# Giving the weight words and the first 26 value products PSUM tiles of their own

## The chip, the cores and the metric

The kernel runs on one core of a Trainium2 chip. The metric is the device time of one launch in microseconds (us); the time before is 849.8 us, the median of three runs (849.23 to 850.05). A difference of 0.2%, about 1.7 us, is roughly what a measurement of this kernel can tell from no change.

## The reference, cut to what matters

The reference is an attention layer followed by a dense layer with a maximum of three products.

```python
# 8 batches, 8 heads, 512 local and 32 global tokens, head size 64
s_g = scale * q_g @ k_all.T;  out_g = softmax(s_g) @ v_all        # global rows see all 544 keys
s_l = concat(scale * q_l @ k_g.T, where(|i-j| <= 32, scale * q_l @ k_l.T, -1e9))
out_l = softmax(s_l) @ concat(v_g, v_l)                           # local rows: globals and a window
x = concat(out_g, out_l) reshaped to 4352 tokens x 512
h = maximum(maximum(x @ w1, x @ w2), x @ w3)                      # 512 -> 768
out = h @ w_out                                                   # 768 -> 512
```

## The kernel before, in words

**Attention by tiles.** A pair of heads has four tiles of 128 local queries; 8 batches times 4 pairs times 4 tiles make 128 tiles. The first 16 are batch 0, taken by halves: `ORDER` (L29) has the first two tiles of all four pairs ahead of the last two of all four. The main loop (L545) makes one tile a turn: `scores` (L325) multiplies queries and keys, takes the mask and the minimum on VectorE (L355), the exponential on ScalarE (L357), and normalises (`times`, L107: L114 on VectorE, L116 on ScalarE, L118 on GpSimd); `trans` (L368) transposes the probabilities on TensorE (L376) into the PSUM tile `T`, which has one buffer, and `copy` (L99: L103 on VectorE, L105 on ScalarE) moves them to `pt`; `glob`, `glob_soft` and `transg` (L279, L303, L387) do the same for the 32 global queries, whose transposed piece is the TensorE instruction `S<-ident,probg` (L394); `pv` (L404) multiplies with the values into the PSUM tile `O` and copies the product to `xr`. The first 26 tiles (`NAT`) use plain float32 operands (L417); later ones use operands split in a high and a low part (L424).

**The dense layer.** `moe_group` (L447) multiplies tokens with weights in split form: `xs` times `wh` and `wl` (L463), the maximum on VectorE (L471), then the high and low part of `h` times `woh` and `wol` (L482). It is a generator; `fill` (L512) takes a few of its matmuls between the steps of a tile. Batch 0 is done in two groups of 256 tokens, the later batches in groups of 512. The first group needs the first eight tiles, the second the next eight.

**The weight pieces.** The weights come as 64-bit floats in 24 pieces of 128 x 512. `convert` (L150) takes a piece through six steps: a DMA into `wraw` (L153, three buffers), the absolute value of the high word on ScalarE (L158, into `wct`), a clamp on GpSimd (L161), three integer operations on VectorE that put together the float32 word (L165, L166, L167), the high part on ScalarE (L170, `wh` or `woh`), the low part on GpSimd (L173, `wl` or `wol`). `weight_step` moves each live piece on by one step. In program order one or two such steps stand in each of the first 18 turns (`WS`, L510).

**Where the words live.** The PSUM pool `psO` has one buffer of 128 x 2 x 512 floats, two halves of 512 columns. It is taken once at the start as `early_o` (L140). L165 and L166 write its second half as the scratch of the words, and L166 and L167 read it. In the same tile, `pv` of the first 18 tiles (`EARLY_O`) writes the first half, in three thirds of 160 columns by turn (L408). From tile 18 on `pv` takes a new `O` of the whole size.

**What sets the order.** The program is written once, in program order; a scheduler then puts each engine's instructions in a fixed row, moving an instruction ahead of others where its operands, as the scheduler sees them, allow, and sets the waits between engines. It follows operands by tile, so what is written in one tile stays in program order there. On the chip each engine works off its row in order and waits where a semaphore says so.

Of the kernel before, what the change touches and what calls it, by code (L numbers as in the profile page):

```python
# [10 lines left out]
F32 = mybir.dt.float32  # L11
F32R = mybir.dt.float32r
I32 = mybir.dt.int32
# [4 lines left out]
PSUM = bass.MemoryType.PSUM  # L18
# [32 lines left out]
def f32(ap):  # L51
    return ap.bitcast(F32)


def body(ctx, tc, kin, qin, vin, min_, win, out):
    nc = tc.nc
    act, dve, pool, pe = nc.scalar, nc.vector, nc.gpsimd, nc.tensor
# [5 lines left out]
    pm = ctx.enter_context(tc.tile_pool(name="pm", bufs=3, space=PSUM))  # L63
    psS = ctx.enter_context(tc.tile_pool(name="psS", bufs=2, space=PSUM))
    psT = ctx.enter_context(tc.tile_pool(name="psT", bufs=1, space=PSUM))
    psO = ctx.enter_context(tc.tile_pool(name="psO", bufs=1, space=PSUM))

    small = ctx.enter_context(tc.tile_pool(name="small", bufs=4))


    load = {"a": 0.0, "d": 0.0, "p": 0.0}

    def width(ap):
        n = 1
        for x in ap.shape[1:]:
            n *= x
        return n

    def spend(e, ns):
        load[e] += ns  # L80

    def least(costs):
        e = min(costs, key=lambda e: load[e] + costs[e])
        load[e] += costs[e]
        return e
# [13 lines left out]
    def copy(out, a, psum=False):  # L99
        n = width(out)  # L100
        c = {"d": n * (1.04 if psum else 0.52) + (160 if psum else 150), "a": n * 0.833 + (150 if psum else 190)}
        if least(c) == "d":
            dve.tensor_copy(out=out, in_=a)  # L103
        else:
            act.copy(out=out, in_=a)  # L105
# [31 lines left out]
    xg = const.tile([128, NP, B, SG], F32, name="xg")  # L137


    early_o = psO.tile([128, 2, 512], F32, name="O")  # L140

    def pieces():
        for n in range(24):
            f, i = divmod(n, 3)
            if n < 18:
                yield n, *[w[f][:, i].rearrange("p k f -> p (k f)") for w in (wh, wl)]
            else:
                yield n, *[w[:, n - 18] for w in wo]

    def convert(piece):  # L150
        m, dh, dl = piece
        r = moe.tile([128, 512], mybir.dt.int64, name="wraw", tag=f"h{3 + m % 3}")
        nc.sync.dma_start(out=r, in_=win[m])  # L153
        hi = r.bitcast(I32).rearrange("p (n t) -> p n t", t=2)[:, :, 1]
        lo = r.bitcast(I32).rearrange("p (n t) -> p n t", t=2)[:, :, 0]
        yield
        c = att.tile([128, 512], I32, name="wct", tag="vs") if m % 2 else moe.tile([128, 512], I32, name="wct", bufs=2)
        act.activation(out=f32(c), in_=r.bitcast(F32).rearrange("p (n t) -> p n t", t=2)[:, :, 1], func=AF.Abs)  # L158
        spend("a", 620)
        yield  # L160
        pool.tensor_scalar(out=f32(c), in0=f32(c), scalar1=HIMAX, scalar2=2.0 ** -15, op0=ALU.min, op1=ALU.max)  # L161
        spend("p", 800)
        yield
        w = early_o[:, 1].bitcast(I32)
        dve.tensor_scalar(out=w, in0=c, scalar1=0x07FFFFFF, scalar2=3, op0=ALU.bitwise_and, op1=ALU.logical_shift_left)  # L165
        dve.scalar_tensor_tensor(out=w, in0=hi, scalar=-0x40000000, in1=w, op0=ALU.bitwise_and, op1=ALU.bitwise_or)  # L166
        dve.scalar_tensor_tensor(out=c, in0=lo, scalar=29, in1=w, op0=ALU.logical_shift_right, op1=ALU.bitwise_or)  # L167
        spend("d", 2000)
        yield
        act.copy(out=dh, in_=f32(c))  # L170
        spend("a", 615)
        yield
        pool.tensor_tensor(out=dl, in0=f32(c), in1=f32(dh), op=ALU.subtract)  # L173
        spend("p", 1290)
        yield True
# [5 lines left out]
    def weight_load():  # L181
        piece = next(todo, None)
        if piece is not None:
            c = convert(piece)
            next(c)
            loaded.append(c)
# [11 lines left out]

    NAT = 26
    EARLY = 16  # L200
    EARLY_O = 18
    kraw, kst, qraw, qs, vraw, vs, xr, sc, pg, pts, pgt = [{} for _ in range(11)]
    prob = []
    kn, qg = [], []
# [199 lines left out]
    def pv(sl):  # L404
        p, t = divmod(ORDER[sl], 4)
        pt = pts.pop(sl)
        if sl < EARLY_O:
            o = early_o[:, :, 160 * (sl % 3):160 * (sl % 3) + 160]  # L408
        else:
            o = psO.tile([128, 2, 512], F32, name="O")  # L410
        if t == 0:
            xr[p] = xp.tile([128, 4, 160], F32, name="xr")
        if sl < NAT:

            for c, j in ((0, 0), (0, 1), (1, 0), (1, 1)):
                n = 160 if c < GCH[t][2] else 128
                pe.matmul(o[64 * j:64 * j + 64, 0, 0:n], lhsT=vraw[sl][:, 2 * j + c], rhs=pt[:, j, c, 0:n], start=(c == 0), stop=(c == 1))  # L417
            copy(xr[p][:, t], o[:, 0, 0:160], True)
        else:

            for j in range(2):
                for c in range(2):
                    n = 160 if c < GCH[t][2] else 128
                    pe.matmul(o[:, j, 0:320].rearrange("p (a q) -> p a q", a=2)[:, :, 0:n],  # L424
                              lhsT=vs[sl][:, 2 * j + c].rearrange("p a d -> p (a d)"),
                              rhs=pt[:, j, c, :, 0:n], start=(c == 0), stop=(c == 1))
            lo = att.tile([64, 2, 160], F32, name="lox", bufs=1)
            copy(lo, o[64:128, :, 0:160], True)
            spend("d", 460 + 2 * 320)
            dve.tensor_tensor(out=lo, in0=o[0:64, :, 160:320], in1=lo, op=ALU.add)  # L430
            for j in range(2):
                dve.tensor_tensor(out=xr[p][64 * j:64 * j + 64, t], in0=o[0:64, j, 0:160], in1=lo[:, j], op=ALU.add)  # L432
        if t == 3:
            dve.tensor_reduce(out=xg[:, p % NP, p // NP], in_=xr[p][:, :, 128:160].rearrange("p t g -> p g t"),
                              axis=AX.X, op=ALU.add)
# [109 lines left out]
    for sl in range(NS):  # L545
        p, t = divmod(ORDER[sl], 4)
# [9 lines left out]
        n = (7, 6, 5, 9) if sl < 16 else (4, 4, 3, 7)  # L556
# [9 lines left out]
        elif sl == 15:  # L566
            load_k(6)
        fill(n[1])
        pv(sl)
        if sl < 8:  # L570
            if p < 3:
# [87 lines left out]
```

## Time and profile before

| | |
|---|---|
| Median of three runs | 849.8 us |
| The profiled execution | 850.82 us, of which the span is 848.8 us |
| TensorE busy | 814.9 us (96%) |
| VectorE, ScalarE, GpSimd busy | 523.8, 530.4, 515.4 us (62, 62, 61%) |
| TensorE idle from 215 us to 840 us | 0.0 us |

The profile names engines PE (TensorE matmuls), PEld (its weight loads), DVE (VectorE), ACT (ScalarE), POOL (GpSimd), SP (the queue that issues DMAs). `L417` is line 417 of the kernel printed above. In a row `[1.99 <-ACT wh L170]` says that the engine sat idle for 1.99 us before this instruction and that a ScalarE instruction of line 170 ended the wait; `x4` counts instructions merged into a row, and a float32 matmul counts twice.

### The profile page before, as it was taken

Reading aid. Unit: us, or ns where it says so; the run is one execution under the profiler, and the core shown is the slowest. Engines: PE = TensorE matmul, PEld = TensorE weight load, DVE = VectorE, ACT = ScalarE, POOL = GpSimd, SP = SyncE. Lnnn points to the kernel's source line nnn. Section 1 sums busy time; section 2 is a strip of 40 time slices with the busy share of each in tenths; the row PEclk is TensorE's granted clock in tenths of the full one; section 3 lists DMA queues with packets and bytes.
Section 4 is the critical chain, followed back from the end, with each engine's and each line's share of the span. In section 5 each row is a group of like instructions: output and inputs, shape, how many; then the busy total and the mean of one; then the engine's idle time right before and its main releaser. Section 6 shows DMA issues by size and latency. Waiting matters only on the chain.

```text
span 848.8 us, 15999 instructions
## 1 busy us (share of the span) xinstructions
PE 814.9 (96%) x4668; PEld 685.8 (81%) x4668; DVE 523.8 (62%) x1784; ACT 530.4 (62%) x1498; POOL 515.4 (61%) x727
## 2 busy tenths in 40 slices
PE   7769889899999999999999999999999999999997
PEld 4558758888888888888888888888888888888896
DVE  4667754677677676767777677676776766421111
ACT  6667665776776777766776776777776676411111
POOL 4677755686768666766678766866676674411211
PEclk9779999999999999999999999999999999999999
DMA  7455545434333433353333433253335322100001
GB/s 262 143 171 190 183 138 150 139 107 146 97 110 94 150 102 101 104 163 113 100 102 114 139 110 109 83 156 100 109 107 161 103 79 72 58 13 1 25 25 26
DMA packets 93415, 94.58 MB, mean 111 GB/s; under 512 B 18448, under 2 KB 81808, under 8 KB 93328
## 3 DMA queue, kind: packets, MB, share of 16 engines
q1 hardware_dynamic: 93328, 93.56, 35.7%
q8 instruction: 38, 0.62, 0.3%
q14 instruction: 49, 0.40, 0.2%
HBM read 56.85 MB, written 8.91 MB: 77 GB/s over the span
## 4 chain that ended last, share of the span: by engine, by line
PE 81%; DVE 2%; DMA 1%; ACT 1%; POOL 1%; issue 1%; SPq 0%; POOLq 0%; ACTq 0%; DVEq 0%
PE pm L463 47%; PE pm L482 15%; PE O L424 6%; PE S L352 5%; PE T L376 4%; PE S L295 2%; DMA prob<-s 1%; PE S L394 1%; PE O L417 1%; PE S L348 1%; ACT s L357 0%; DVE xr L432 0%; DVE pt L97 0%; ACT sg L308 0%; DVE s L355 0%
## 5 line engine op out<-in xcount | busy, mean ns | idle before, releaser
L463 PE MATMUL pm<-xs,wh 128*128 128x512 f32 (+1 forms) x1440 | 419.9, 367 | 2.7 <-ACT wh L170 2.4
L463 PEld LDWEIGHTS pm<-xs,wh 128*128 128x128 f32 x1440 | 252.6, 189 | 33.3 <-ACT wh L170 2.9
L463 PE MATMUL pm<-xs,wl 128*128 128x512 f32 (+1 forms) x720 | 266.0, 370 | 3.9 <-POOL wl L173 3.8
L463 PEld LDWEIGHTS pm<-xs,wl 128*128 128x128 f32 x720 | 136.1, 189 | 25.7 <-POOL wl L173 5.2
L118 POOL TENSOR_SCALAR s<-s,z 128x224 f32<-128x224 f32 (+1 forms) x246 | 105.6, 442 | 63.8 <-ACT lox L105 40.6
L482 PE MATMUL pm<-woh,h 128*128 128x512 f32 x408 | 133.9, 399 | 1.0 <-POOL h L97 1.0
L357 ACT ACTIVATE s<-s,nm 128x224 f32<-128x224 f32 (+1 forms) x256 | 118.2, 463 | 18.8 <-DVE nm L355 14.5
L97 POOL TENSOR_TENSOR h<-m,h 128x512 fp32r<-128x512 f32 (+1 forms) x60 | 68.7, 1145 | 99.0 <-ACT h L105 98.7
L471 DVE TENSOR_TENSOR m<-pm,m 128x512 f32<-128x512 f32 (+1 forms) x120 | 73.0, 608 | 77.6 <-PE pm L463 75.5
L97 POOL TENSOR_TENSOR qs<-qraw,qs 128x256 fp32r<-128x256 f32 x100 | 73.2, 740 | 62.6 <-ACT qs L105 54.3
L97 DVE TENSOR_TENSOR pt<-T,pt 128x512 fp32r<-128x512 f32 x102 | 70.5, 691 | 63.2 <-ACT pt L105 61.9
L355 DVE CUSTOM_DVE_ANT_0 s<-S,mask 128x224 f32<-128x224 f32 (+1 forms) x240 | 80.6, 371 | 30.2 <-PE S L348 23.8
L482 PEld LDWEIGHTS pm<-woh,h 128*128 128x128 f32 x408 | 74.3, 188 | 13.7 <-POOL h L97 1.6
L482 PE MATMUL pm<-wol,h 128*128 128x512 f32 x204 | 82.3, 404 | 2.5 <-POOL wol L173 2.5
L97 POOL TENSOR_TENSOR vs<-vraw,vs 128x256 fp32r<-128x256 f32 x102 | 75.8, 744 | 6.5 <-ACT vs L105 3.3
L97 POOL TENSOR_TENSOR kst<-kraw,kst 64x576 fp32r<-64x576 f32 x50 | 71.6, 1433 | 13.2 <-issue 6.3
L105 ACT CAST pt<-T 128x512 fp32r<-128x512 f32 x88 | 51.3, 583 | 40.7 <-PE T L376 40.6
L105 ACT CAST qs<-qraw 128x256 fp32r<-128x256 f32 x99 | 40.2, 407 | 53.6 <-PE S L352 52.0
L424 PEld LDWEIGHTS O<-pt,vs 128*128 128x128 f32 x408 | 66.1, 188 | 8.8
L424 PE MATMUL O<-pt,vs 128*128 128x320 f32 (+1 forms) x408 | 72.8, 300 | 0.0
L432 DVE TENSOR_TENSOR xr<-O,lox 64x160 f32<-64x160 f32 x204 | 64.3, 315 | 3.4
L352 PEld LDWEIGHTS S<-kst,qs 128*128 128x128 f32 x400 | 59.5, 190 | 8.5 <-DVE nmg L299 0.2
(97 smaller groups left out, 1228.1 us busy)
## 6 DMA issues: line engine op xcount, KB each, us to landing
vraw<-v_in SPq DMA_DIRECT2D x64, 256.0 KB, 3.2
qraw<-q_in SPq DMA_DIRECT2D x100, 128.0 KB, 2.2
prob<-s SPq DMA_DIRECT2D x56, 224.0 KB, 2.4
wraw<-w_in SPq DMA_DIRECT2D x24, 512.0 KB, 3.4
prob<-s SPq DMA_DIRECT2D x56, 192.0 KB, 2.3
out_dram<-o SPq DMA_DIRECT2D x32, 256.0 KB, 2.5
kraw<-k_in SPq DMA_DIRECT2D x25, 320.0 KB, 3.0
qn<-q_in SPq DMA_DIRECT2D x8, 256.0 KB, 6.0
```

What stands on the lines that cost most here:

```text
L97: (dve if least(c) == "d" else pool).tensor_tensor(out=out, in0=a, in1=b, op=ALU.subtract)
L105: act.copy(out=out, in_=a)
L118: pool.tensor_scalar(out=out, in0=a, scalar1=col, scalar2=1.0, op0=ALU.mult, op1=ALU.mult)
L352: pe.matmul(ph[j][:, 0:n], lhsT=qs[i][:, a, 128 * j:128 * j + 128], rhs=kst[p][:, j, c0:c0 + n], start=(a == 0), stop=(a == 1))
L355: dve.tensor_tensor_reduce(out=s[:, j, 0:n], in0=ph[j][:, 0:n], in1=mask[:, (1, 0, 1, 0)[t], 32 * (t == 0):32 * (t == 0) + n], scale=-0.12 ...
L357: act.activation(out=s[:, j, 0:n], in_=s[:, j, 0:n], func=AF.Exp, bias=nm[:, j:j + 1], scale=-1.0, accum_out=ze[:, j, 0:1])
L376: pe.transpose(pr[:, 256 * j + 128 * c:256 * j + 128 * c + 128], s[:, j, 128 * c:128 * c + 128], one)
L424: pe.matmul(o[:, j, 0:320].rearrange("p (a q) -> p a q", a=2)[:, :, 0:n], lhsT=vs[sl][:, 2 * j + c].rearrange("p a d -> p (a d)"), rhs=pt[ ...
L432: dve.tensor_tensor(out=xr[p][64 * j:64 * j + 64, t], in0=o[0:64, j, 0:160], in1=lo[:, j], op=ALU.add)
L463: pe.matmul(ps[:, 0:n], lhsT=w[f][:, i, k], rhs=xs[k][:, a, c0:c0 + n], start=(q == 0), stop=(q == 11))
L471: dve.tensor_tensor(out=m[:, 0:n], in0=ps[:, 0:n], in1=m[:, 0:n], op=ALU.max)
L482: pe.matmul(ps, lhsT=hh[f][:, a, 128 * t:128 * t + 128], rhs=w[:, f], start=(q == 0), stop=(q == 17))
```

## The change

The pool `psO` and the tile `early_o` go from the start of the program. A pool `psE` takes their place, with two tiles of one buffer each: `W`, 128 x 512 integers, taken anew by every weight piece, and `O`, 128 x 160 floats, taken anew by `pv` of each of the first 26 tiles. Each takes one PSUM bank (the place of a 512-column float32 tile, of which `psO` took two). At tile 26 `psE` is closed and `psO` is opened in its place for the later tiles. So the value products no longer go round three thirds of one bank but take one place by turn, and no tile is shared with the words. Instructions, operands, DMAs and the engine on which each stands are the same in number and shape; their order in the rows of the engines is not. Lines after the edit shift by one or two (L463 is L465 after, L417 is L419).

```diff
-    psO = ctx.enter_context(tc.tile_pool(name="psO", bufs=1, space=PSUM))
+    first = ctx.enter_context(ExitStack())
+    psE = first.enter_context(tc.tile_pool(name="psE", bufs=1, space=PSUM))
+    psO = []
...
-    early_o = psO.tile([128, 2, 512], F32, name="O")
...
-        w = early_o[:, 1].bitcast(I32)
+        w = psE.tile([128, 512], I32, name="W")
         dve.tensor_scalar(out=w, in0=c, scalar1=0x07FFFFFF, scalar2=3, op0=ALU.bitwise_and, op1=ALU.logical_shift_left)
...
-        if sl < EARLY_O:
-            o = early_o[:, :, 160 * (sl % 3):160 * (sl % 3) + 160]
-        else:
-            o = psO.tile([128, 2, 512], F32, name="O")
+        if sl < NAT:
+            o = psE.tile([128, 160], F32, name="O")
+        else:
+            if not psO:
+                first.close()
+                psO.append(ctx.enter_context(tc.tile_pool(name="psO", bufs=1, space=PSUM)))
+            o = psO[0].tile([128, 2, 512], F32, name="O")
...
-                pe.matmul(o[64 * j:64 * j + 64, 0, 0:n], lhsT=vraw[sl][:, 2 * j + c], rhs=pt[:, j, c, 0:n], start=(c == 0), stop=(c == 1))
-            copy(xr[p][:, t], o[:, 0, 0:160], True)
+                pe.matmul(o[64 * j:64 * j + 64, 0:n], lhsT=vraw[sl][:, 2 * j + c], rhs=pt[:, j, c, 0:n], start=(c == 0), stop=(c == 1))
+            copy(xr[p][:, t], o, True)
```

On TensorE the rows of the two programs differ between the first group's first matmuls and the product of tile 20; from there to the end they are the same, instruction for instruction. The rows below, in the prediction, show three places of the difference.

More of the change, by code (lines that the diff above doesn't have):

```diff
@@ L200, in body @@
     EARLY = 16
-    EARLY_O = 18
     kraw, kst, qraw, qs, vraw, vs, xr, sc, pg, pts, pgt = [{} for _ in range(11)]
```

## The prediction

> **What bounds the kernel now.** I read the page first, then the stretches, who waited for whom, and the timelines of the engines in the stretches that came out. The page's busy line and its clock row:
>
> ```profile
> span 848.8 us, 15999 instructions
> PE 814.9 (96%) x4668; PEld 685.8 (81%) x4668; DVE 523.8 (62%) x1784; ACT 530.4 (62%) x1498; POOL 515.4 (61%) x727
> PEclk9779999999999999999999999999999999999999
> ```
>
> PE bounds the whole, and the clock dips only in the second and third slice. The stretches, with PE's busy time as the second number and the granted clock as the one behind the last engine:
>
> ```profile
> 21.00:45.20 24.20, 15.98 (x79) 11.13 (x80) 16.03 (x57) 15.30 (x46) 15.95 (x29) 0.75 0.49 150
> 45.20:64.00 18.80, 14.31 (x76) 11.16 (x77) 11.00 (x35) 12.55 (x38) 13.00 (x20) 0.77 0.55 172
> 64.00:85.00 21.00, 20.61 (x165) 18.50 (x164) 15.54 (x41) 14.57 (x39) 16.93 (x23) 1.00 0.57 187
> 85.00:95.00 10.00, 9.24 (x67) 7.91 (x66) 8.21 (x24) 7.36 (x19) 7.44 (x11) 1.00 0.55 168
> 95.00:106.00 11.00, 8.79 (x62) 6.96 (x61) 7.41 (x23) 7.16 (x20) 7.47 (x10) 1.00 0.65 199
> 106.00:119.00 13.00, 10.81 (x57) 6.86 (x54) 9.54 (x25) 8.38 (x23) 8.30 (x10) 1.00 0.56 180
> 119.00:127.00 8.00, 7.05 (x51) 4.39 (x53) 1.80 (x10) 5.37 (x14) 3.46 (x5) 1.00 0.21 63
> 127.00:148.00 21.00, 20.85 (x172) 18.47 (x169) 10.05 (x49) 11.89 (x40) 10.97 (x17) 1.00 0.52 156
> 215.00:840.00 625.00, 625.00 (x3448) 532.12 (x3446) 386.05 (x1293) 386.65 (x1078) 372.82 (x511) 1.00 0.31 95
> ```
>
> From 215 us on PE is never idle, and the changed order meets the old one at the product of tile 20 (about 131 us). So the change is worth what PE gains before 131 us, one for one. What there is to gain: idle of 8.2 us (24.20 - 15.98) from 21 to 45, 4.5 (18.80 - 14.31) to 64, 0.4 to 85, and 6.1 from 85 to 127. To this comes the clock: 30.3 us of PE work (15.98 + 14.31) at 0.76 would be about 23 at 1.00, 7.2 us more. All together some 26 us; ahead of 21 us the two orders differ hardly. Who is waited for, in the first 260 us:
>
> ```profile
> PE S L394 <- POOL probg L118: 4.2, 2, 2.5
> PE pm L463 <- POOL wl L173: 3.8, 5, 1.2
> PE pm L482 <- POOL wol L173: 2.5, 5, 0.9
> PE pm L463 <- ACT wh L170: 2.4, 2, 2.0
> PE T L376 <- ACT pt L105: 1.9, 3, 1.3
> PE O L417 <- DVE wct L167: 1.4, 2, 1.1
> ```
>
> Weight pieces that come late (8.7 us in three rows) cost more than the products that wait for a piece's words (1.4, the last row).
>
> **First place: the first words.** VectorE, from the transposed piece of pair 1 on (`pt<-S`), before:
>
> ```order
> L103 COPY pt<-S 128x2x32 [waits PE_49]
> L360 RECIPROCAL z<-z 128x2 [waits DVE_49]
> L299 ISA sg,nmg<-S,zero 64x384 [waits PE_49,Pool_49]
> L299 ISA nmg 64x1
> L359 TENSOR_REDUCE z<-z_92 128x2 [waits Activation_49]
> L299 ISA sg,nmg<-S,zero 64x160 [waits PE_49]
> L299 ISA nmg 64x1
> L165 TENSOR_SCALAR O<-wct 128x512 [waits Activation_49]
> ```
>
> VectorE in the new order, where the first words stand ahead of tile 6's scores (L354) and of all of the above:
>
> ```order
> L165 TENSOR_SCALAR W<-wct 128x512 [waits Pool_49]
> L354 ISA s_94,nm<-pm,mask 128x192 [waits PE_49]
> L354 ISA nm 128x1
> L358 TENSOR_REDUCE z<-z_92 128x2 [waits Activation_49]
> L105 COPY pt<-T 128x4x128 [waits PE_49]
> L359 RECIPROCAL z<-z 128x2 [waits DVE_49]
> L105 CAST xs<-xr 128x256 [waits Activation_49]
> L308 TENSOR_SCALAR zg<-zg 64x1 [waits Activation_49]
> L354 ISA s_94,nm<-pm,mask 128x192
> L354 ISA nm 128x1
> L309 RECIPROCAL zg<-zg 64x1 [waits DVE_49]
> L166 SCALAR_TENSOR_TENSOR W<-wraw,W 128x512 [waits DMAHW1_49]
> ```
>
> The wait on ScalarE (the copy out of `O`) is gone, and the words moved 24 rows up. The trace has the clamped piece long before it is used (POOL, DVE, and what PE waits for behind it):
>
> ```profile
> 18.51 0.61 POOL L161 TENSOR_SCALAR wct<-wct 128x512 f32<-128x512 f32 x1
> 27.02 0.68 DVE L165 TENSOR_SCALAR O<-wct 128x512 int32<-128x512 int32 x1
> 29.85 0.79 PE L463 MATMUL pm<-xs,wh 128*128 128x256 f32 x2 [1.99 <-ACT wh L170]
> 31.21 0.58 PE L463 MATMUL pm<-xs,wl 128*128 128x256 f32 x1 [0.57 <-POOL wl L173]
> 41.43 0.39 PE L463 MATMUL pm<-xs,wl 128*128 128x256 f32 x1 [1.16 <-POOL wl L173]
> 45.13 0.48 PE L394 MATMUL S<-ident,probg 128*128 128x128 f32 x1 [2.51 <-POOL probg L118]
> ```
>
> The clamp ends at 19.1 and L165 starts at 27.0: the first piece can be some 5 us earlier, so I cost the waits of 1.99, 0.57 and 1.16 at nothing afterwards: -3.7. The price stands on GpSimd, whose row up to the normalised global probabilities of pair 2 was, before:
>
> ```order
> L118 TENSOR_SCALAR s_94<-s_94,z 128x224 [waits DVE_49,Activation_49]
> L118 TENSOR_SCALAR s_94<-s_94,z 128x224 [waits Activation_49]
> L173 TENSOR_TENSOR wl_104<-wct,wh_98 128x512 [waits Activation_49]
> L118 TENSOR_SCALAR probg<-sg,zg 64x128 [waits DVE_49,Pool_49]
> L118 TENSOR_SCALAR probg<-sg,zg 64x96 x2
> ```
>
> and is now, from the same piece 0's low part on:
>
> ```order
> L173 TENSOR_TENSOR wl_104<-wct,wh_98 128x512 [waits Activation_49]
> L99 TENSOR_TENSOR xs<-xr,xs 128x256 [waits Activation_49]
> L161 TENSOR_SCALAR wct<-wct 128x512 [waits Activation_49]
> L173 TENSOR_TENSOR wl_104<-wct,wh_98 128x512 [waits DVE_49,Activation_49]
> L120 TENSOR_SCALAR s_94<-s_94,z 128x224 [waits DVE_49,PE_49]
> L120 TENSOR_SCALAR s_94<-s_94,z 128x224 [waits PE_49]
> L120 TENSOR_SCALAR probg<-sg,zg 64x128 [waits DVE_49,Pool_49]
> L120 TENSOR_SCALAR probg<-sg,zg 64x96 x2
> ```
>
> An `xs`, a clamp and a second low part moved ahead of `probg`, which PE's `S<-ident,probg` waits for. Their durations:
>
> ```profile
> 35.78 0.61 POOL L161 TENSOR_SCALAR wct<-wct 128x512 f32<-128x512 f32 x1 [1.64 <-ACT wct L158]
> 36.36 0.74 POOL L97 TENSOR_TENSOR xs<-xr,xs 128x256 fp32r<-128x256 f32 x1
> 32.88 1.26 POOL L173 TENSOR_TENSOR wl<-wct,wh 128x512 fp32r<-128x512 f32 x1 [0.73 <-ACT wh L170]
> ```
>
> 0.61 + 0.74 + 1.26 = 2.6 us. PE has work moved ahead of that wait (below), but it runs out: I charge all 2.6. The 2.51 us at 45.13 has the same chain behind it, and I leave it. First term: **-3.7 + 2.6 = -1.1 us**, bounds +2.6 (nothing saved) and -6.2 (1.99 + 0.57 + 1.16 + 2.51, all gone and the price hidden).
>
> **Second place: the products.** TensorE behind the global piece of pair 1, before (`O_113` is `early_o`, the product that of tile 3):
>
> ```order
> L376 MATMUL T_429<-ident_82,s4_94 128x128 [waits Activation_49]
> L376 MATMUL T_429<-ident_82,s4_94 128x128 x3
> L463 MATMUL pm_657<-xs_314,wh0_98 128x256 [waits Activation_49]
> L463 MATMUL pm_657<-xs_314,wh0_98 128x256
> L463 MATMUL pm_657<-xs_314,wl0_104 128x256 [waits Pool_49]
> L394 MATMUL S_413<-ident_82,probg_405 128x128 [waits Activation_49,Pool_49]
> L348 MATMUL S_436<-kn_114,qn_243 128x224 [waits DMAHW5_49,PE_49]
> L348 MATMUL S_436<-kn_114,qn_243 128x224
> L417 MATMUL O_113<-pt_322,vraw_181 64x160 [waits DVE_49]
> ```
>
> and now (`O_400` is the same product):
>
> ```order
> L465 MATMUL pm_674<-xs_315,wh0_98 128x256 [waits Activation_49]
> L465 MATMUL pm_674<-xs_315,wh0_98 128x256
> L465 MATMUL pm_674<-xs_315,wl0_104 128x256 [waits Pool_49]
> L375 MATMUL T_435<-ident_82,s4_94 128x128 [waits Activation_49]
> L375 MATMUL T_435<-ident_82,s4_94 128x128
> L419 MATMUL O_400<-pt_323,vraw_180 64x160 [waits Activation_49]
> L419 MATMUL O_400<-pt_323,vraw_180 64x160 x3
> ```
>
> The product moved ahead of pair 2's global piece, and waits for the copy out of `O` in place of the words on VectorE. What the old wait cost, and what came of it:
>
> ```profile
> 55.50 0.71 PE L417 MATMUL O<-pt,vraw 128*64 128x160 f32 x8 [1.12 <-DVE wct L167]
> 57.53 1.12 PE L376 MATMUL T<-ident,s 128*128 128x128 f32 x4 [1.31 <-ACT pt L105]
> ```
>
> The second wait is the first's child: the copy of `pt` stands on ScalarE behind the copy out of `O`. Second term: 1.12 + 1.31 + 0.28 (the rest of the 1.4 above) = **-2.7 us**; if the copy out of `O` is late in place of the words, 0.
>
> **The clock.** The same four half-products, with the idle time before them:
>
> ```profile
> 45.40 1.70 PE L348 MATMUL S<-kn,qn 128*128 128x224 f32 x4
> 51.55 0.93 PE L348 MATMUL S<-kn,qn 128*128 128x224 f32 x4
> ```
>
> Right behind the 2.51 us wait they take 1.70 us, six microseconds later 0.93: after waits of this size PE runs at half speed for some 4 us. Four waits bring these 7.2 us (the two for `probg`, 4.2 in all, that at 29.85 and those at 55 to 57); two of them go, one new one comes on `probg`: a quarter, **-1.8 us**; bounds 0 and -7.2. The Trainium skill, "TensorE: Matmul & The Clock Gate", Part 1 (the HAM clock gate), throttles after an idle window of about 3.4 us; no single wait here is that long and the slow matmuls are there all the same, so the measurement decides. By the page's figure alone this term would be 0 and the sum 1.8 us smaller.
>
> **The later weight pieces.** Between 64 and 215 us PE waits for pieces like this:
>
> ```profile
> PE pm L482 <- POOL wol L173: 2.5, 5, 0.9
> PE pm L463 <- POOL wl L173: 2.0, 3, 1.0
> PE pm L463 <- ACT wh L170: 0.4, 1, 0.4
> ```
>
> Together 4.9 us. The pieces come in pairs between two products. First words of the pairs' first pieces, and the last piece's last:
>
> ```profile
> 61.40 0.70 DVE L165 TENSOR_SCALAR O<-wct 128x512 int32<-128x512 int32 x1 [0.80 <-POOL wl L173]
> 99.18 0.69 DVE L165 TENSOR_SCALAR O<-wct 128x512 int32<-128x512 int32 x1 [0.92 <-ACT xr L105]
> 119.65 0.68 DVE L167 SCALAR_TENSOR_TENSOR wct<-wraw,O 128x512 int32<-128x512 int32 x1
> ```
>
> Ten pieces lie between the first two rows, 3.8 us a piece, and the second shows the words waiting for the copy out of `O`. Without that tie GpSimd is next: in 64 to 85 us, 5.5 pieces at this pace, it is 16.93 us busy, 3.1 a piece. Over the last 15 pieces 0.7 us each would cover all 4.9 us; a pace that stays covers none. I take half: **-2.5 us**.
>
> **New waits.** Freed rows make new ones: half a wait of the largest size seen, 2.51: **+1.2 us** (0 to 2.5). At tile 26 the new pool waits for copies that are long done: nothing.
>
> Sum: -1.1 - 2.7 - 1.8 - 2.5 + 1.2 = **-6.9 us**, so the profiled execution's 850.8 (its span of 848.8 and 2.0 around it) would be 843.9; it lies 1.0 above the median of the runs, and the median of 849.8 becomes **842.9**.
>
> **The rivals.** *The tie was the whole lock.* If the early waits go too (-6.2), the products' (-2.7), half the clock (-3.6) and all weight waits (-4.9), with one new wait of 2.5, it is -14.9: 834.9; from half of what is beyond my forecast on, about -10, I count it here. For it: between 21 and 127 us no engine is full. Against: GpSimd is 81% busy in the best stretch. Chance 0.20. *The tie hides behind the pieces.* PE gets its work at the pace of the pieces, and their pace is that of the chain of DMA and five engine steps: then the last two terms give nothing and the clock little: -0.5 to -4, around 847.5. For it: direct waits on the words are 1.4 us only. Chance 0.20. *Slower: weight work ahead of `probg`.* GpSimd and VectorE now take words first, and PE's row stops at `S<-ident,probg`, with everything queued behind. If both such waits (pairs 2 and 3) grow by 2.6 us, each brings 4 us at half speed (2 us lost), and the products' 2.7 is all that is saved: 5.2 + 4 - 2.7 = +6.5, 856.3. It decides from the point at which these two waits, with their slow clock, outgrow 7 us. Against: PE has work moved ahead, and the pieces are early. Chance 0.10. The forecast itself, -4 to -10, has 0.50. That the change does nothing is out: the rows differ.
>
> **How the numbers follow.** Faster by over 1.7 us (0.2%): 0.50 + 0.20 + 0.10 of the second rival = 0.80; within: 0.11, the second rival's rest and the slower rival's edge; slower: 0.09. The range 836 to 849.5 leaves out the far end of the first rival and what is slower, some 0.2 together.
>
> **What would show it.** In the changed profile: no wait of `O` for `wct` (second term); the first L465 before 29 us without a wait for `wh`, and `S<-ident,probg` of pair 2 waiting for GpSimd (first); the clock in 21 to 64 us above 0.80; the waits for `wl` and `wol` halved and the last L167 ahead of 113 us; the product of tile 20 near 124 instead of 131 us, and the same time from there to the end. Wrong is the forecast if PE's idle time ahead of 127 us is what it was.

## The result, and the profile after

The changed kernel takes 836.43 us (median of four runs, 835.65 to 837.12) against 849.92 us of the kernel before (849.23 to 851.57, four runs): ratio 0.9838, 95% interval 0.9821 to 0.9855, a gain of 13.5 us. The forecast was 842.9, a gain of 6.9; the result lies at the low end of the range of 836 to 849.5, 0.4 us inside it. The profiled execution took 835.65 us, 15.2 less than the profiled one of before, and its span is 15.3 us shorter. The page after:

```profile
span 833.5 us, 15973 instructions
PE 807.3 (97%) x4668; PEld 684.4 (82%) x4668; DVE 522.6 (63%) x1784; ACT 528.3 (63%) x1498; POOL 513.9 (62%) x727
PEclk9899999999999999999999999999999999999999
```

PE runs the same 4668 matmuls in 7.6 us less busy time and is idle 26.2 us instead of 33.9. The third slice of the clock is at 0.9 or more, the second at 0.8, both 0.7 before. Four of the stretches of the prediction (PE busy second, the clock behind the last engine):

```profile
21.00:45.20 24.20, 17.98 (x94) 12.23 (x93) 18.59 (x61) 17.48 (x52) 17.95 (x31) 0.83 0.60 188
45.20:64.00 18.80, 16.04 (x121) 13.40 (x122) 14.58 (x46) 15.35 (x47) 16.58 (x26) 0.95 0.66 221
64.00:85.00 21.00, 21.00 (x174) 19.28 (x170) 18.57 (x51) 17.14 (x47) 19.60 (x25) 1.00 0.72 229
200.00:820.00 620.00, 620.00 (x3425) 528.50 (x3424) 385.47 (x1292) 386.29 (x1077) 371.33 (x509) 1.00 0.31 96
```

Stretches of equal time hold more work now (121 matmuls instead of 76 from 45.2 to 64), so the gain is read at equal points of the work. PE from the start to the product of tile 19 (the 20th), from which on its two rows are alike, first before, then after:

```profile
0.00:131.02 131.02, 106.03 (x650) 80.65 (x650) 80.80 (x278) 85.89 (x243) 82.66 (x130) 0.92 0.57 183
```

```profile
0.00:116.40 116.40, 98.91 (x650) 78.86 (x651) 79.61 (x278) 83.78 (x243) 81.91 (x130) 0.96 0.64 206
```

After 650 matmuls in both, the changed kernel is 14.6 us ahead: 7.1 of PE's busy time (106.03 - 98.91) and 7.5 of its idle time (24.99 - 17.49). From there to the end both take nearly the same time, 717.8 and 717.1 us. A point on the way, at nearly equal counts of matmuls, before and then after:

```profile
0.00:64.00 64.00, 45.52 (x228) 32.58 (x229) 36.50 (x149) 41.19 (x125) 38.18 (x72) 0.84 0.60 193
```

```profile
0.00:56.26 56.26, 42.10 (x229) 29.52 (x229) 36.65 (x144) 38.63 (x117) 36.90 (x70) 0.91 0.68 226
```

The 228th matmul comes 7.7 us earlier, the 650th 14.6: a half of the gain comes in the stretch of the first pieces, the other 6.9 us later. Of these 6.9, 3.2 are idle time (6.5 of PE behind the first row, 3.3 behind the second) and 3.7 busy time (60.5 and 56.8). (The kinds of matmul among the first 228 aren't quite the same in both, so the split is rough.) Who is waited for in the first 260 us:

```profile
PE S L393 <- POOL probg L120: 2.3, 1, 2.3
PE pm L465 <- ACT xs L107: 2.3, 2, 1.5
PE pm L465 <- POOL xs L99: 2.2, 2, 1.8
PE O L419 <- ACT pt L107: 1.2, 1, 1.2
PE pm L484 <- POOL wol L173: 1.2, 2, 0.7
PE pm L465 <- ACT wh L170: 1.0, 1, 1.0
PE pm L465 <- POOL wl L173: 0.2, 1, 0.2
```

The weight pieces, 8.7 us in three rows before, are down to 2.4; in their place stands `xs`, the split tokens, with 4.5. The words themselves, VectorE's instructions on the tile (min, median and max duration in ns, then first and last start), before and after:

```profile
L165 DVE TENSOR_SCALAR O<-wct x24: 680/690/696, 27.0 to 117.3; 128x512 int32<-128x512 int32 x24
L167 DVE SCALAR_TENSOR_TENSOR wct<-wraw,O x24: 673/686/690, 28.5 to 119.6; 128x512 int32<-128x512 int32 x24
```

```profile
L165 DVE TENSOR_SCALAR W<-wct x24: 674/694/696, 19.1 to 100.2; 128x512 int32<-128x512 int32 x24
L167 DVE SCALAR_TENSOR_TENSOR wct<-wraw,W x24: 669/680/689, 23.4 to 101.8; 128x512 int32<-128x512 int32 x24
```

They take as long as before, but start 8 us earlier and end 17.8 us earlier.

### The profile page after: what moved, and what is told of

Its sections match the earlier page's. It is cut to its first block, busy times and chain, and to the rows that moved or that the text cites. A ratio compares the mean times of both kernels' runs of the same rounds, so it can differ in the third digit from the quotient of the medians.

```text
span 833.5 us, 15973 instructions
## 1 busy us (share of the span) xinstructions
PE 807.3 (97%) x4668; PEld 684.4 (82%) x4668; DVE 522.6 (63%) x1784; ACT 528.3 (63%) x1498; POOL 513.9 (62%) x727
## 4 chain that ended last, share of the span: by engine, by line
PE 83%; DVE 1%; POOL 1%; issue 1%; ACT 1%; DMA 0%; POOLq 0%; DVEq 0%; ACTq 0%
PE pm L465 48%; PE pm L484 16%; PE O L426 6%; PE S L351 5%; PE T L375 4%; PE S L294 2%; PE S L393 1%; PE S L347 1%; PE O L419 1%; DMA prob<-s 0%; ACT s L356 0%; DVE kst L105 0%; POOL s L120 0%; DVE xr L434 0%; DVE sg L298 0%
## 5 line engine op out<-in xcount | busy, mean ns | idle before, releaser
L465 PE MATMUL pm<-xs,wh 128*128 128x512 f32 (+1 forms) x1440 | 422.0, 368 | 5.7 <-ACT xs L107 2.3
L465 PEld LDWEIGHTS pm<-xs,wh 128*128 128x128 f32 x1440 | 253.3, 189 | 36.4 <-ACT xs L107 2.7
L465 PE MATMUL pm<-xs,wl 128*128 128x512 f32 (+1 forms) x720 | 265.1, 368 | 0.2 <-POOL wl L173 0.2
L465 PEld LDWEIGHTS pm<-xs,wl 128*128 128x128 f32 x720 | 136.3, 189 | 20.6 <-issue 1.6
```

The lines of the kernel that those rows point to most:

```text
L465: pe.matmul(ps[:, 0:n], lhsT=w[f][:, i, k], rhs=xs[k][:, a, c0:c0 + n], start=(q == 0), stop=(q == 11))
```

## The experiments

The tie between words and products can act in three ways: by where the values lie (one bank or two, three thirds or one place), by the waits at run time (a product waits for words, words wait for a copy), or by the order in which it makes the scheduler put each engine's instructions. The first two runs tell these apart; the next parts ask which part of the order brings the gain. Each ratio is to runs of the kernel before on the same chip.

**The tie put back by hand, the tiles as in the change.** Each of the first 19 products waits for the words ahead of it, and each L165 for the last copy out of `O`; all engines' rows are then those of before, instruction for instruction. (`mi` in the code is a product's matmul.)

```diff
-        dve.tensor_scalar(out=w, in0=c, scalar1=0x07FFFFFF, scalar2=3, op0=ALU.bitwise_and, op1=ALU.logical_shift_left)
+        behind(dve.tensor_scalar(out=w, in0=c, scalar1=0x07FFFFFF, scalar2=3, op0=ALU.bitwise_and, op1=ALU.logical_shift_left), "o")
...
-        dve.scalar_tensor_tensor(out=c, in0=lo, scalar=29, in1=w, op0=ALU.logical_shift_right, op1=ALU.bitwise_or)
+        tie["w"] = dve.scalar_tensor_tensor(out=c, in0=lo, scalar=29, in1=w, op0=ALU.logical_shift_right, op1=ALU.bitwise_or)
...
+                if sl <= 18:
+                    behind(mi, "w")
+            tie["o"] = copy(xr[p][:, t], o, True)
```

> Words and products in PSUM tiles of their own as after the change, but the tie put back by hand: each product of the first 19 tiles waits for the words written ahead of it in program order, and each piece's first words wait for the copy out of the product ahead of them. The rows of all engines are those of before, instruction for instruction. Tie theory (the gain comes from untying words and products): the time of before, 849 to 851 us. Rival, the PSUM place (a bank for each, and one place for the products in place of three thirds, is itself the gain): 836 to 838.

Measured: 850.40 us, ratio 1.0007 (0.9991 to 1.0023). All of the gain is gone with the tie back, so where the values lie is worth nothing that these runs can measure.

**The old rows without the tie.** Up to the product of tile 20 every engine's row is held as it was before, by edges that set an order within an engine and no wait between engines. (`ROWS` has the old rows, one list for each engine; `done` finds an instruction by its name.)

```diff
+    for row in ROWS:
+        row = [f"I-{n}" for n in row if f"I-{n}" in done]
+        for x, y in zip(row, row[1:]):
+            tc.add_manual_dep(done[y], x, mybir.DependencyInfo(mybir.DependencyClass.NoSync, mybir.DependencyReason.DATA), reason="row")
```

> The tiles of the change with no tie at all, but the rows of all engines held in the order of before up to the product of tile 20, so that only the waits between words and products are gone. Order theory (the tie cost by what the scheduler had to make of it: words and products in fixed turns, in rows that each engine works off): little gain, 1 to 4 us, 846 to 849. Rival, the waits theory (the order is as good, the waits on the chip cost): most of the 13.5 us, 836 to 840.

Measured: 849.70 us, ratio 0.9997 (0.9980 to 1.0013). The waits on it (a helper records these kernels, so every line is L75):

```profile
PE pm L75 <- POOL wl L75: 4.0, 5, 1.1
PE T L75 <- ACT pt L75: 2.8, 2, 2.5
PE pm L75 <- ACT wh L75: 2.5, 2, 1.9
PE pm L75 <- POOL wol L75: 1.8, 3, 0.9
```

No product waits for `wct` any more, and the waits for weight pieces are there as before (8.3 us). `T` waits 2.8 us for `pt` instead of 1.9. The time is that of before, 0.7 us above what the order theory expected. The 1.4 us that the trace of before lists under the tie's name bring nothing that shows by themselves: what the change gains is the order.

**Which engine's order.** First PE's row alone held as before (`ROWS[3]`), the other engines free; then the other engines' rows held and PE free.

```diff
-    for row in ROWS:
+    for row in ROWS[3:4]:
```

> The change, with TensorE's row held in the order of before up to the product of tile 20 and the other engines' rows left to the scheduler. If TensorE's row decides (a product stands behind much dense work, and the next tile behind it): 846 to 852. If the rows of the others decide (words late on VectorE, pieces late): 836 to 842.

```diff
-    for row in ROWS:
+    for row in ROWS[:3] + ROWS[4:]:
```

> The converse: the rows of VectorE, ScalarE, GpSimd and the DMA queue held in the order of before, TensorE's left to the scheduler. If TensorE's row decides: 836 to 843. If the others' rows decide: 846 to 852.

Measured: 843.48 us, ratio 0.9923 (0.9903 to 0.9943), and 855.08 us, ratio 1.0063 (1.0041 to 1.0085). In the first, with PE's old row, the last of the words, PE's longest wait in its timeline, and the stretch around it:

```profile
L75 DVE SCALAR_TENSOR_TENSOR wct<-wraw,W x24: 664/682/689, 23.4 to 101.7; 128x512 int32<-128x512 int32 x24
```

```profile
34.08 0.47 PE L75 MATMUL S<-ident,probg 128*128 128x128 f32 x1 [4.75 <-POOL probg L75]
```

```profile
21.00:45.20 24.20, 16.38 (x78) 11.18 (x78) 19.28 (x63) 16.16 (x47) 18.03 (x29) 0.65 0.58 191
```

In the second, with the others' old rows, the last of the words and two of PE's waits:

```profile
L75 DVE SCALAR_TENSOR_TENSOR wct<-wraw,W x24: 673/686/690, 26.9 to 118.5; 128x512 int32<-128x512 int32 x24
```

```profile
PE pm L75 <- POOL wl L75: 5.6, 5, 1.8
...
PE O L75 <- ACT xr L75: 4.2, 3, 2.5
```

The first lies between its two expectations, the second is slower than both of its. With PE's old row the pieces are as early as in the change (last L167 at 101.7, there 101.8), and half the gain is there, 6.7 us; but PE stands 4.75 us at the `probg` of pair 2, with nothing moved ahead of it, and its clock falls to 0.65 from 21 to 45 us. With the others' old rows the pieces come as late as ever, and the kernel is 4.9 us slower than before.

The two runs don't cut the change's order in two, though, for the rows left free don't come out as those of the change. In the first, VectorE's and GpSimd's rows leave those of the change from about 30 us on. In the second, PE's row is a new one: 490 of its first 650 matmuls stand in one order with the change's row, no more to speak of than the 479 of the row before. So what the change's own PE row is worth by itself is not shown; shown is that early pieces with PE's old row bring half, and that a PE row made anew beside late pieces brings a loss.

**The pace of the pieces.** The change with two `wraw` buffers in place of three, so that each piece's DMA starts later.

```diff
-        r = moe.tile([128, 512], mybir.dt.int64, name="wraw", tag=f"h{3 + m % 3}")
+        r = moe.tile([128, 512], mybir.dt.int64, name="wraw", tag=f"h{3 + m % 2}")
```

> The change with two buffers for the landed weight pieces in place of three, so that the pieces come slower: a landing of 3.3 us and some 5 us of steps behind it, over two buffers about 4 us a piece in place of 2.7. If the pace of the pieces carries the gain: 845 to 850. If the pieces are early enough anyway: 836 to 840.

Measured: 856.95 us, ratio 1.0084 (1.0064 to 1.0104). PE's waits for pieces, and the first words of a piece:

```profile
PE pm L465 <- POOL wl L173: 6.2, 8, 1.2
PE pm L465 <- ACT wh L170: 4.1, 5, 1.2
PE pm L484 <- POOL wol L173: 4.1, 4, 1.9
```

```profile
L165 DVE TENSOR_SCALAR W<-wct x24: 673/694/696, 18.9 to 136.1; 128x512 int32<-128x512 int32 x24
```

From first to last the words take 117.2 us over 23 steps, 5.1 us a piece, where the change takes 3.5 ((100.2 - 19.1) / 23) and before took 3.9 ((117.3 - 27.0) / 23). The waits for pieces come to 14.4 us, and the kernel is 20 us slower than the change, slower than both expectations. The pieces are late here even against before, and the rows are other ones again. So the run shows that PE lives on the pace of the pieces; what the untied order would be worth at the old pace it doesn't show.

**Half the tie.** The tie put back by hand for the last 15 pieces only (shown against the run with all of it back), and then for the first 9 only (`m < 9`).

```diff
-        behind(dve.tensor_scalar(out=w, in0=c, scalar1=0x07FFFFFF, scalar2=3, op0=ALU.bitwise_and, op1=ALU.logical_shift_left), "o")
+        behind(dve.tensor_scalar(out=w, in0=c, scalar1=0x07FFFFFF, scalar2=3, op0=ALU.bitwise_and, op1=ALU.logical_shift_left), "o" if m >= 9 else "none")
...
-        tie["w"] = dve.scalar_tensor_tensor(out=c, in0=lo, scalar=29, in1=w, op0=ALU.logical_shift_right, op1=ALU.bitwise_or)
+        tie["w" if m >= 9 else "free"] = dve.scalar_tensor_tensor(out=c, in0=lo, scalar=29, in1=w, op0=ALU.logical_shift_right, op1=ALU.bitwise_or)
```

> Words and products in PSUM tiles of their own; the tie put back by hand for the last 15 pieces only, the first 9 are free. Nothing else differs from the change, and no words lie in SBUF. If the gain comes in two parts (by the matmul counts of the profiles of before and after, 7.7 us ahead of the place that before reaches at 64 us, the rest behind it): 842 to 844. If only the whole gains: 848 to 852.

> The converse, the first 9 pieces tied and the last 15 free. Two parts: about 7 us, 842 to 845. The prediction's term for the later pieces alone, 2.5 us: 847. Only the whole gains: 848 to 852.

Measured: 845.02 us, ratio 0.9944 (0.9927 to 0.9962), with the first 9 free (1 us above what was expected for a gain in two parts), and 844.86 us, ratio 0.9942 (0.9923 to 0.9960), with the last 15 free. Both halves carry, 5.2 and 5.3 us; the two sum to 10.5 of the 13.5. The other 3 us would come only with both, but each of the three gains is known to some 1.5 us only, so that these 3 are hardly clear of noise.

**The words apart, but in SBUF.** In the kernel before, the words' scratch moved to an SBUF tile, for the first 9 pieces, for the last 15 (`m >= 9`), and for all (no condition):

```diff
-        w = early_o[:, 1].bitcast(I32)
+        w = moe.tile([128, 512], I32, name="W", tag="o", bufs=2) if m < 9 else early_o[:, 1].bitcast(I32)
```

> The kernel before, with the words of the first 9 pieces in an SBUF tile of their own (two buffers, the place of the output tile) and those of the other 15 still in the products' tile. Both theories of the order: by the matmul counts of the two profiles 7.7 of the 14.6 us are won by the place that before reaches at 64 us: about 842. By the terms of the prediction (first, second and clock term, 5.6 us): 844. If the early pieces only shift the wait to the later ones: 848 to 850.

> The converse: the first 9 pieces' words in the products' tile, the last 15 in an SBUF tile of their own. By the matmul counts some 7 us are won behind the place that before reaches at 64 us: about 843. By the term of the prediction (2.5 us for the later pieces): 847.5. If the pace is set at the start alone: 849 to 850.

> The kernel before with the words of all 24 pieces in an SBUF tile of their own (two buffers, the place of the output tile); products stay in the thirds of their shared tile. If untying gains whatever the rows come to: 836 to 840. If it is these rows, those that the scheduler happened to make for the PSUM tiles, that gain: anywhere from 842 to 858, as the two half-untied kernels (849 and 858) did.

Measured: 849.15 us, ratio 0.9992 (0.9979 to 1.0004); 858.28 us, ratio 1.0099 (1.0071 to 1.0128); 861.88 us, ratio 1.0137 (1.0115 to 1.0159). The last two are slower than every time expected for them. These runs didn't separate what they were made to separate, since the place has a price of its own. The words in the last of them (min, median and max):

```profile
L166 DVE SCALAR_TENSOR_TENSOR W<-wraw,W x24: 674/836/3046, 21.3 to 120.7; 128x512 int32<-128x512 int32 x24
L165 DVE TENSOR_SCALAR W<-wct x24: 395/427/1490, 19.2 to 118.9; 128x512 int32<-128x512 int32 x24
```

With the words in SBUF, L166 takes 674 ns at best and 3046 at worst, 1141 on average where it takes 691 after the change, and GpSimd's clamp 741 ns instead of 614. Though untied, the last L165 starts at 118.9 us, as late as before (117.3). The gain of the free order and this price can't be told apart in these three, and the two runs with half the tie above took their place.

**Can the pieces go faster still?** In the changed kernel GpSimd is 16.58 of 18.80 and 19.60 of 21.00 us busy in the two best stretches. One run moves the clamp (L161) from GpSimd to VectorE, one takes two piece steps in every turn.

```diff
-        pool.tensor_scalar(out=f32(c), in0=f32(c), scalar1=HIMAX, scalar2=2.0 ** -15, op0=ALU.min, op1=ALU.max)
-        spend("p", 800)
+        dve.tensor_scalar(out=f32(c), in0=f32(c), scalar1=HIMAX, scalar2=2.0 ** -15, op0=ALU.min, op1=ALU.max)
+        spend("d", 420)
```

> The change, with the clamp of the weight pieces (L161) moved from GpSimd to VectorE. In the changed profile GpSimd is 88% and 93% busy from 45 to 64 and 64 to 85 us, VectorE 78% and 88%. If GpSimd now bounds the start: 0.61 us less for each piece there, 2 to 4 us faster than the change, 832 to 834.5. If VectorE is as full, or the two engines slow each other in SBUF: 836 to 842.

```diff
-    WS = [1, 1, 2, 1, 2, 2, 1, 2] + [2] * 8 + [1] * 2
+    WS = [2] * 15
```

> The change, with two weight steps in each of the first 15 turns in place of one or two in the first 18, so that pieces come earlier in program order. If earlier pieces still gain: 833 to 836. If the start is full and they push the tiles back: 837 to 845.

Measured: 844.36 us, ratio 0.9936 (0.9919 to 0.9954), and 842.46 us, ratio 0.9911 (0.9897 to 0.9926): 8 and 6 us slower than the change, the first also slower than both of its expectations. In the first the words end later (the last L167 starts at 107.2), in the second a little earlier (101.0) than in the change (101.8), and there PE waits for something else:

```profile
PE pm L465 <- ACT xs L107: 3.5, 2, 3.1
```

Every such edit also changes the rows of all engines, so neither run says what a faster GpSimd alone would bring. None of the kernels was faster than the change.

## Why the prediction was right, and where it was not

**The bound: right.** From 200 us on PE is never idle, and the gain at the product of tile 19 (14.6 us) is the gain of the span (15.3) but for 0.7. What the prediction calls the product of tile 20, at about 131 us, is the 20th product, tile 19's when counted from 0: it was to come near 124 us and comes at 116.4.

**First term (-1.1): about -4.5; the saving nearly right, the price on GpSimd not paid where I put it.** The first L465 starts at 27.03 with no wait, as foretold, where before one at 29.85 had waited 1.99 us:

```profile
23.74 0.48 PE L393 MATMUL S<-ident,probg 128*128 128x128 f32 x1 [2.27 <-POOL probg L120]
...
27.03 0.48 PE L465 MATMUL pm<-xs,wh 128*128 128x256 f32 x2
...
34.77 0.48 PE L393 MATMUL S<-ident,probg 128*128 128x128 f32 x1
...
43.59 0.30 PE L393 MATMUL S<-ident,probg 128*128 128x128 f32 x1
```

Of the 3.7 us saved there 1.2 are back, 0.96 at 32.09 for `wh` and 0.22 at 33.46 for `wl`. I had charged 2.6 us because GpSimd has more to do ahead of pair 2's `probg`. At 34.77, where pair 2's piece stands, there is no wait: the matmuls moved ahead of it on PE cover the price. The 2.51 us in front of the next pair (43.59) are gone as well, which I had left in. The one `probg` wait left is pair 1's, 2.27 where it was 1.74. That makes -3.7 + 1.2 - 2.5 + 0.5 = -4.5. The price itself was real. GpSimd starts this `probg` 3.2 us later than before (first row before, second after), and before PE took the piece at 31.59 (third row):

```profile
31.13 1.01 POOL L118 TENSOR_SCALAR probg<-sg,zg 64x128 f32<-64x128 f32 x3
34.35 1.00 POOL L120 TENSOR_SCALAR probg<-sg,zg 64x128 f32<-64x128 f32 x3
31.59 0.44 PE L394 MATMUL S<-ident,probg 128*128 128x128 f32 x1
```

In the run with PE's old row, with no matmuls moved ahead, PE takes it at 34.08: 2.5 us later than before, close to the 2.6 charged. (The wait in front of it is longer, 4.75 us, because PE comes there sooner, without the old waits for the first piece.) So it was the cover, said to run out, that held. The slower rival needed this wait and the next to grow; its mechanism is seen in that run alone, and even there the kernel is 6.7 us faster than before.

**Second term (-2.7): about -2.** No product waits for `wct`. One waits 1.2 us for the copy of `pt` that it needs (row above), and the waits of `T` for `pt`, 1.9 us, are gone: (1.4 + 1.9) - 1.2 = 2.1.

**The clock (-1.8): about -3.9.** The traces show at which times the clock was at half speed: before, 23.06 to 26.47, 29.89 to 36.72, 43.54 to 50.37 and 57.20 to 60.61 us; after, 23.30 to 26.71, 33.54 to 36.95 and 43.78 to 47.19. The sums over these pieces, before and after:

```profile
sum 20.48, PE 17.65 PEld 12.67 DVE 9.00 ACT 10.74 POOL 15.53; mean PE 4.41 PEld 3.17 DVE 2.25 ACT 2.68 POOL 3.88
```

```profile
sum 10.23, PE 9.79 PEld 7.08 DVE 4.58 ACT 4.95 POOL 9.95; mean PE 3.26 PEld 2.36 DVE 1.53 ACT 1.65 POOL 3.32
```

PE was busy for 17.65 us at half speed, now for 9.79; half of each is lost, 8.8 and 4.9. (The 7.2 of the prediction is too small: it weighs the clock by time, and PE is busier in the slow pieces than between them.) More came back than the quarter that I had taken, above all from 45 to 64 us, whose mean is 0.95 where it was 0.77. What half speed costs is seen in two equal groups of the changed kernel, the first right behind a wait of 1.49 us:

```profile
42.90 0.62 PE L465 MATMUL pm<-xs,wh 128*128 128x256 f32 x3 [1.49 <-ACT xs L107]
...
43.72 1.75 PE L347 MATMUL S<-kn,qn 128*128 128x224 f32 x4
...
62.06 0.92 PE L347 MATMUL S<-kn,qn 128*128 128x224 f32 x4
```

The Trainium skill, "TensorE: Matmul & The Clock Gate", Part 1 (the HAM clock gate), throttles after an idle window of about 3.4 us; here, as before, no wait from 21 us on is that long (2.27 at most) and the slow groups are there, so the page's figure would have left out this term, and the measurement speaks against using it as a limit on single waits.

**The later weight pieces (-2.5): -3.7 of the waits, and 6.9 us in this stretch.** The mechanism came true as written. From the ninth words (51.06, before 61.40) to the nineteenth (82.43) a piece takes 3.1 us ((82.43 - 51.06) / 10, rows below), the figure that I had worked out from GpSimd's work, and of the 4.9 us of waits for pieces after 64 us one row of 1.2 is left (`wol`, above):

```profile
51.06 0.67 DVE L165 TENSOR_SCALAR W<-wct 128x512 int32<-128x512 int32 x1
...
82.43 0.69 DVE L165 TENSOR_SCALAR W<-wct 128x512 int32<-128x512 int32 x1
```

So three quarters went where I took half. My own figures spoke for more than half: 0.7 us for each of 15 pieces is 10.5 us, twice what the waits needed. Other waits took 2.0 of it back (`O` for `pt`, 1.2, and `T` for `xr`, 0.8), and all idle time behind the 228th matmul fell by 3.2 us. The other 3.7 of the 6.9 are busy time at full clock, for which the prediction had no term.

**New waits (+1.2): 4.5 us** on `xs`, more than I had allowed for (2.5).

**Busy time: the term that was missing.** PE's busy time fell by 7.1 us to the product of tile 19, and the clock explains 3.9 of it. Most of the rest goes with the stops. The record of a matmul in a stream lasts 0.28 us, but the next one starts 0.12 us behind it:

```profile
47.57 0.28 PE L465 MATMUL pm<-xs,wl 128*128 128x256 f32 x1
47.69 0.28 PE L465 MATMUL pm<-xs,wh 128*128 128x256 f32 x1
```

The last matmul ahead of a stop has no follower and counts whole, some 0.16 us more. Up to the product of tile 19 PE's records fall into 33 unbroken stretches before and into 19 after (behind the 228th matmul, 15 and 5). By this estimate (the ends of matmuls are modelled in the profile) 14 stops fewer are some 2 of the 3.2 us that the clock leaves; the last 1 us stays open. A wait that goes takes with it its idle time, the end of the matmul ahead of it and, at times, a piece of slow clock; the prediction charged the first and the last.

Put together, the terms measured are -4.5, -2.1, -3.9, -3.7 and +4.5, -9.7 us; with 3.2 of busy time and 1.7 of smaller waits that went they make the 14.6.

**The rivals.** "The tie was the whole lock", 834.9, had the nearer number, and by the prediction's own count a gain beyond some 10 us is this rival's: with 13.5 the forecast itself, 4 to 10, came out too small, and its range held only at its edge. The rival's list (early waits, products, half the clock, all weight waits, one new wait) names what happened; its chance of 0.20 was too low. That its sum comes so near is partly luck: its terms as measured come to -9.7, and the 5.2 us too much in them stand in for the busy time and the smaller waits, which it doesn't have. I held against it that GpSimd is 81% busy in the best stretch; it went to 93% (19.60 of 21.00), and the pieces came faster. "The tie hides behind the pieces" falls: with the tie gone the words end 17.8 us earlier. That PE lives on the pace of the pieces was right, as the two `wraw` buffers show.

## What to carry to other kernels

A tile shared by unrelated values is a dependency for the scheduler, and its cost lies in the order that it forces on every engine, not in the waits listed under its name (1.4 us listed, 13.5 gained, and nothing measurable when the waits went and the order stayed). Look at how far the rows move when the tie goes, and bound the gain by all idle time, lost clock and stops ahead of the point where the rows meet again, not by the waits of the operands that get earlier. When a feeder gets earlier, check that the consumer's row moves with it: here early pieces with PE's old row gave half of the gain.

## What the runs showed of the hardware that was not expected

The place of a scratch tile set the speed of two engines. With both operands in SBUF, L166 took 1141 ns on average and up to 3046, against 691 with one operand in PSUM; L165, which only writes there, was faster at best (395 ns against 674) and slower at worst (1490 against 696); GpSimd's clamp went from 614 to 741 ns. The Trainium skill, "SBUF — State Buffer", Who interferes with whom, says that a VectorE instruction with two SBUF inputs contends with a GpSimd instruction that reads SBUF, the second to start being held until the first is done. The traces agree: with no GpSimd instruction beside it L166 takes 0.68 us (at 40.41), and beside a `wl` that has 1.11 us to go it takes 1.65, to 0.54 us behind the end of the `wl`:

```profile
90.81 1.47 POOL L173 TENSOR_TENSOR wl<-wct,wh 128x512 fp32r<-128x512 f32 x1
91.17 1.65 DVE L166 SCALAR_TENSOR_TENSOR W<-wraw,W 128x512 int32<-128x512 int32 x1
```

It can also be the GpSimd instruction that is held: a 128x192 product of `s` that starts at 46.29, behind an L167 at 46.02 and beside an L166 at 46.67, takes 1.27 us, where such a product takes 0.43 on average after the change.

PE lost its full clock behind waits as short as 1.5 us (43.72 above: 1.75 us for four matmuls that take 0.92 later), but a longer wait, 1.76 us in front of 55.24, cost none. In these traces the clock changes in pieces of 3.41 us on a fixed grid, and what counts is PE's idle time within a piece. Three pieces of the changed kernel (PE busy second, the clock behind the last engine):

```profile
40.37:43.78 3.41, 1.85 (x17) 1.22 (x13) 3.38 (x13) 3.36 (x13) 1.99 (x6) 1.00 0.70 224
43.78:47.19 3.41, 3.41 (x16) 2.40 (x16) 2.18 (x7) 2.52 (x8) 3.41 (x5) 0.50 0.75 245
54.02:57.43 3.41, 2.06 (x14) 1.86 (x14) 1.71 (x5) 1.58 (x6) 3.24 (x6) 1.00 0.68 261
```

The first is idle for 1.56 us, and the second, right behind it, runs at half speed. The wait in front of 55.24 falls into two pieces; the third row, which has the larger part, is idle for 1.35 us, and the piece behind it stays at 1.00. In all the traces here, up to 200 us, a full-speed piece with less than 1.3 us idle never lost the clock, one with more than 1.9 always did, and between the two it went either way.
